# Decode attention with 32 K and V tiles on one core: the output weights' first 16 heads in 20 KB rows, and 0/1 matrices built earlier on GpSimd

## The chip, the core and the metric

One core of a Trainium2 chip runs the whole kernel. The metric is the device time of one execution in microseconds; the figures of a kernel are the median, the lowest and the highest of its runs. Engines: TensorE (PE: matmuls; PEld: its weight loads), VectorE (DVE), ScalarE (ACT), GpSimd (POOL) and SyncE (SP, which here only issues loads). Sixteen DMA engines move the data.

## The reference

One token for each of 8 sequences passes an attention layer with a K and V cache and, beside it, a small MLP. Shapes: D = 640, 32 heads of 128, 4096 keys, F = 1728, all bfloat16.

```python
def _A_ref(x, k_cache, v_cache, wq, wo):
    q = (x @ wq).reshape(B, Sq, Hq, Dh).transpose(0, 2, 1, 3)
    scores = jnp.einsum("bhqd,bhkd->bhqk", q, k_cache) * (Dh ** -0.5)
    p = softmax(scores)
    o = jnp.einsum("bhqk,bhkd->bhqd", p, v_cache)
    return o.transpose(0, 2, 1, 3).reshape(B, Sq, Hq * Dh) @ wo

def _B_ref(x, w1, b1, w2, b2):
    y = _layernorm(x)
    return gelu(y @ w1 + b1) @ w2 + b2

xn = _layernorm(A_x)
return A_x + _A_ref(xn, ...) + _B_ref(xn, ...)
```

The caches hold 8 x 32 x 4096 x 128 values each: 268 MB of K and 268 MB of V. Each is read once.

## The kernel before

**Tiles.** The work is cut into 32 turns (`NQ`). Turn i holds 8 heads (`HS`) of one sequence: i = 8 hq + b, so heads 0 to 7 of all sequences come first and heads 24 to 31 last. A K or V tile of a turn is 128 partitions x 256 keys x 128 values, 8.4 MB, in rows of 64 KB. Partition p holds keys of head p // 16, so eight heads lie side by side in the partitions. There are three slots of this size: KA (K of even turns), KB (K of odd turns) and VS (V of every turn).

**A turn.** K times q is split between two engines. 80 of the 256 keys per partition go over TensorE: `pe_T` transposes them, `act_T` (ScalarE) copies them out of PSUM, `pe_QK` multiplies with q, and `dve_sel` keeps the right head with a mask. The other 176 go over VectorE in three chunks (`dve_chunk`): a product with q in place (`TENSOR_TENSOR`, two operands in SBUF), an add of the two halves (another such), and a reduce over what is left. `dve_max` finds the maxima, `act_exp` makes the exponentials and their sums, `pe_RS` adds the sums over the partitions, `dve_rinv` inverts them, `pe_PV` does 256 matmuls against V, and GpSimd's `o_norm` writes the normalised result of the turn into `oT_sb` (head dimension in the partitions, one column for each head and sequence). The turns overlap: `pe_RS` and `pe_PV` of turn i lie behind the transposes and scores of turn i + 1. In the last turn (31) `o_norm` is done by VectorE.

**Order.** The order of the instructions on each engine is written out by hand. Each step is given a position with `at(pos, fn, ...)`, the steps are sorted by position (turn i begins at 100 i), and each one appends its instructions to the queues of its engines. `o` in the last lines is 3200, behind the last turn. Waits are on semaphores and stand in the queues in the same order, so that an engine that waits holds up all that is behind in its queue.

**GpSimd's queue in a turn.** `qrep` (a copy of q, repeated, 128x128), `o_norm` of the turn before the last, and `k_ready`: a memset of one column that waits for the landing of K and lets TensorE start on it. At its start GpSimd makes constants and iotas (`consts_pool`).

**The output projection.** wo has 4096 rows (32 heads of 128) of 640 values. The contraction runs over the partitions of wo as it is laid out in SBUF. `load_wl(0)` brings heads 0 to 15 as two blocks of 8 heads: in each block partition p holds 8 neighbouring rows of wo, 10 KB in one piece; a block's row p * 8 + s belongs to head p // 16 of the block, at value (p % 16) * 8 + s. `load_wl(1)` brings heads 16 to 23 the same way, and three `load_wn` heads 24 to 31 in three column pieces. They go into the slot KA once K of turn 30 is used up: the waits in `load_wl` are for the last transposes and the last product of K(30) (`tk[("kt", 30)]`, `tk[("km", 30)]`). In SP's queue `load_wl(0)` stands behind V(30) and ahead of the four pieces of V(31); `load_wl(1)` and `load_wn` stand behind those.

Since wo's rows are spread this way, `oT_sb` has to be turned to match: for each s the value (p % 16) * 8 + s of head p // 16 must come to partition p. `sel_pool` (GpSimd) builds 0/1 matrices for this in KA, 8 of 128x128, from the identity. `pe_sel` multiplies them with `oT_sb` of three blocks of heads in four PSUM banks, and `dve_fold` multiplies with a mask (`mask_sb`, one head in 16 partitions) and adds over the heads into `oS_sb`. `pe_sel3` and `dve_fold3` do the same for heads 24 to 31, in two parts: sequences 0 to 6, and, after the last turn, sequence 7. `fin_wl` and `fin_wn` are the projection's matmuls; they add into `ACC_ps`, which already holds x, b2 and the MLP. `fin_store` casts, transposes and stores.

In GpSimd's queue `sel_pool` stands at position 3199, behind the last `o_norm` that GpSimd does (turn 30, position 3175):

Of the kernel before, what the change touches and what calls it, by code (L numbers as in the profile page):

```python
# [14 lines left out]
P = 128  # L15
# [176 lines left out]
def bass_parallel_sum__gqa_block_cached__mixer_channel_mlp__decode_kernel(  # L192
# [17 lines left out]
    HS = 8  # L210
# [13 lines left out]
    KA, KB, VS = 0, 1, 2  # L224
    WL_CUT = (0, 2, 3)
    WN_CUT = (0, 5, 7, HS)
# [21 lines left out]
    with ExitStack() as es:  # L248
# [12 lines left out]
        w1_sb = part(VS, DC * H * DH, DC * F).rearrange("p (c n) -> p c n", c=DC)  # L261
        NL = WL_CUT[-1]
        woL_sb = part(KA, 0, NHQ * HS * D).rearrange("p (g x) -> p g x", g=NHQ)
        sel_sb = part(KA, H * D, HS * P).rearrange("p (c h r) -> p c h r", c=HS, h=HS)
        o_ = [0]
# [16 lines left out]
        iota_h = scratch(2 * HS).bitcast(I32)  # L282
        mtmp = scratch(2 * 2 * HS).bitcast(F32).rearrange("p (w n) -> p w n", w=2)
        ones_sb = scratch(B, 1)
        zeros_sb = scratch(P)
# [8 lines left out]
        oT_sb = sb("oT_sb", [P, H, B], BF)  # L294
        oS_sb = sb("oS_sb", [P, HS, NL, B], BF)
        oS3_sb = sb("oS3_sb", [P, HS, B], BF)
        oU_sb = sb("oU_sb", [P, 2, HS], F32)
        ident_bf = sb("ident_bf", [P, P], BF)
        mask_sb = sb("mask_sb", [P, HS], F32)
        off_sb = sb("off_sb", [P, HS], F32)  # L300
        mx_sb = sb("mx_sb", [P, 32], F32)
# [32 lines left out]
        ld_k0 = _Dma(sem("ld_k0"))  # L334
        ld_wl = [_Dma(sem(f"ld_wl{q}")) for q in range(len(WL_CUT) - 1)]
        ld_wn = [_Dma(sem(f"ld_wn{q}")) for q in range(len(WN_CUT) - 1)]
# [38 lines left out]
        def load_wl(q):  # L375
            sp.wait(tk[("kt", NQ - 2)], tk[("km", NQ - 2)])
            lo, hi = WL_CUT[q], WL_CUT[q + 1]
            n = HS * DH
            tk[("wl", q)] = ld_wl[q].sig(sp.dma_start(
                woL_sb[:, lo:hi, :],  # L380
                A_wo[lo * n:hi * n, :].rearrange("(g p s) n -> p g (s n)", p=P, s=HS)))

        def load_wn(q):
            lo, hi = WN_CUT[q], WN_CUT[q + 1]
            n = HS * DH
            tk[("wn", q)] = ld_wn[q].sig(sp.dma_start(
                woL_sb[:, NL, lo * D:hi * D],
                A_wo[NL * n:(NL + 1) * n, :].rearrange("(p s) n -> p (s n)", p=P)[:, lo * D:hi * D]))

        def consts_pool():  # L390
            pool.iota(iota_h, [[-HP, HS]], base=0, channel_multiplier=1)
            tk["iota"] = pool.sig(pool.iota(iota_i, [[1, P]], base=0, channel_multiplier=-1))
            for d, (ap, v) in zip([None] + ld_vl, (
                    (zeros_sb, 0.0), (ones_sb, 1.0), (mx_sb[:, :], 0.0), (mb_sb[:, :], 0.0))):
                inst = pool.memset(ap, v)
                if d is not None:
                    inst.call[3] = (d.sem, 1)
            tk["consts"] = pool.sig(pool.memset(ones_f[:, :], 1.0))

        def sel_pool():  # L400
            pool.wait(tk["id"], tk[("kt", NQ - 2)], tk[("km", NQ - 2)])
            tk["sel"] = pool.sig(pool.tensor_copy(
                sel_sb[:, :, :, :],
                ident_bf[:, :].rearrange("p (r c) -> p c r", c=HS)[:, :, None, :].to_broadcast([P, HS, HS, HP])))
# [20 lines left out]
        def idents():  # L425
            dve.wait(tk["iota"])
            tk["id"] = dve.sig(dve.tensor_scalar(ident_bf[:, :], iota_i, 0.0, None, ALU.is_equal))
            dve.tensor_scalar(mtmp[:, 0, :], iota_h, 0.0, None, ALU.is_ge)
            t = dve.sig(dve.tensor_scalar(mtmp[:, 1, :], iota_h, float(HP), None, ALU.is_lt))
            dve.wait(t)  # L430
            t = dve.sig(dve.tensor_tensor(mask_sb[:, :], mtmp[:, 0, :], mtmp[:, 1, :], ALU.mult))
            dve.wait(t)
            tk["mask"] = dve.sig(dve.tensor_scalar(off_sb[:, :], mask_sb[:, :], 1.0, 1e30, ALU.subtract, ALU.mult))

        def pe_xT(w):
# [237 lines left out]

        def pe_sel(n):
            ap, bank = sel_bank(n)
            pe.wait(tk["sel"], *[tk[("on", i)] for i in range(NL * B)])
            bank.use(pe)
            w = HS * B
            for x in range(2 * NL):
                c, g = divmod(x, NL)  # L680
                last = pe.matmul(ap[:, x * w:(x + 1) * w],
                                 sel_sb[:, 2 * n + c, :, :].rearrange("p h r -> p (h r)"),
                                 oT_sb[:, g * HS:(g + 1) * HS, :].rearrange("p h b -> p (h b)"),
                                 start=True, stop=True)
            bank.used(pe, pe.sig(last))

        def dve_fold(n):
            ap, bank = sel_bank(n)
            bank.use(dve)
            view = ap[:, 0:2 * NL * HS * B].rearrange("p (x h b) -> p x h b", h=HS, b=B)  # L690
            t = dve.sig(dve.tensor_tensor(
                view, view, mask_sb[:, None, :, None].to_broadcast([P, 2 * NL, HS, B]), ALU.mult))
            dve.wait(t)
            tk[("oS", n)] = bank.used(dve, dve.sig(dve.tensor_reduce(
                oS_sb[:, 2 * n:2 * n + 2, :, :].rearrange("p s g b -> p (s g) b"),
                view.rearrange("p x h b -> p x b h"), AX.X, ALU.add)))

        def sel3_b(n):
            return (0, B - 1, QB_ps[:, :], QBB) if n == 0 else (B - 1, B, S_ps[:, 0, :], SBK[0])

        def pe_sel3(n):
            lo, hi, ap, bank = sel3_b(n)
            pe.wait(tk["sel"], *[tk[("on", NL * B + b)] for b in range(lo, hi)])
            bank.use(pe)
            view = ap[:, 0:HS * HS * (hi - lo)].rearrange("p (h s b) -> p h s b", h=HS, s=HS)
            for c in range(HS):
                last = pe.matmul(view[:, :, c, :], sel_sb[:, c, :, :].rearrange("p h r -> p (h r)"),
                                 oT_sb[:, NL * HS:H, lo:hi], start=True, stop=True)
            bank.used(pe, pe.sig(last))

        def dve_fold3(n):
            lo, hi, ap, bank = sel3_b(n)
            w = HS * (hi - lo)
            bank.use(dve)
            view = ap[:, 0:HS * w].rearrange("p (h x) -> p h x", h=HS)
            t = dve.sig(dve.tensor_tensor(
                view, view, mask_sb[:, :, None].to_broadcast([P, HS, w]), ALU.mult))
            dve.wait(t)
            tk[("oS3", n)] = bank.used(dve, dve.sig(dve.tensor_reduce(
                oS3_sb[:, :, lo:hi], view.rearrange("p h (s b) -> p s b h", s=HS), AX.X, ALU.add)))  # L720

        def fin_wl(q):
            lo, hi = WL_CUT[q], WL_CUT[q + 1]
            pe.wait(tk[("wl", q)], *[tk[("oS", n)] for n in range(HS // 2)])
            for g in range(lo, hi):
                for r in range(HS):
                    for c in range(DC):
                        pe.matmul(ACC_ps[:, c * B:(c + 1) * B], woL_sb[:, g, r * D + c * P:r * D + (c + 1) * P],
                                  oS_sb[:, r, g, :], start=False, stop=False, skip_group_check=True)

        def fin_wn(q):
            lo, hi = WN_CUT[q], WN_CUT[q + 1]
            pe.wait(tk[("wn", q)], tk[("oS3", 0)], tk[("oS3", 1)])
            for r in range(lo, hi):
                for c in range(DC):
                    last = pe.matmul(ACC_ps[:, c * B:(c + 1) * B],
                                     woL_sb[:, NL, r * D + c * P:r * D + (c + 1) * P], oS3_sb[:, r, :],
                                     start=False, stop=(r == HS - 1), skip_group_check=True)
# [27 lines left out]
        at(-795, idents)  # L766
        at(NQ * Q - 1, sel_pool)
        at(-790, norm, 0)
        at(-780, pe_xT, 0)
        at(-775, cp_xT, 0)  # L770
        at(-774, norm, 1)
# [40 lines left out]
        o = NQ * Q  # L812
        for q in range(len(WL_CUT) - 1):
            at(o - 55 if q == 0 else o + 50 + 0.1 * q, load_wl, q)
            at(o + 79.1 + 0.2 * q, fin_wl, q)
        for q in range(len(WN_CUT) - 1):
            at(o + 51 + q, load_wn, q)
            at(o + 80 + q, fin_wn, q)
        for n in range(HS // 2):
            at(o + n, pe_sel, n)  # L820
            at(o + 0.5 + n, dve_fold, n)
        for n in range(2):
            at(o + 5 if n == 0 else o + 79.2, pe_sel3, n)
            at(o + 5.5 if n == 0 else o + 79.5, dve_fold3, n)
        at(o + 90, fin_store)
# [72 lines left out]
```

## Time and profile before

| | |
|---|---|
| median of 3 runs | 1283.74 us (1283.46 to 1283.85) |
| profiled execution: time | 1283.28 us |
| profiled execution: span | 1281.7 us |
| TensorE's granted clock, mean | 0.588 |
| read from HBM | 551.80 MB, 431 GB/s over the span |
| busy share: DMA engines, nearly every slice | 0.9 or more |
| busy: VectorE | 1094.9 us (85%) |
| busy: TensorE matmuls | 669.8 us (52%) |
| busy: ScalarE | 475.5 us (37%) |
| busy: GpSimd | 92.1 us (7%) |
| K(31) lands, VectorE starts on it | 1227.32 us |
| last wo piece that the chain of waits names lands | 1277.36 us |

The span goes from the first to the last instruction of the program on the core; the time of an execution holds some more around it (1.6 us here). Times below with two decimals are microseconds from the span's start. In a line of the timeline stand: start, duration, engine, line, operation, output <- inputs, shapes, number of instructions, and in brackets the idle time of the engine just before, with what ended it. All of the work has line 111, that of a helper which records every operation, so operations are told apart by their tiles. `S_sb` is the memory of the three slots, so K, V and all that is put into them for a time (the weights, the 0/1 matrices) bear that name.

### The profile page before, as it was taken

How to read it: one execution, taken by the hardware profiler on the slowest of the kernel's cores; microseconds unless marked ns; L12 is line 12 of the kernel's file. 1: busy time of each engine (PE TensorE's matmuls, PEld its weight loads, DVE VectorE, ACT ScalarE, POOL GpSimd, SP SyncE). 2: the span in 40 equal slices, each digit the busy share in tenths (PEclk: the TensorE clock that was granted, in tenths of full speed). 3: DMA queues.
4: the chain of work that ended last, by engine and by line, in shares of the span. 5: the costliest groups of instructions: out<-in, count | busy, mean ns of one | idle time of the engine just before them, and what ended most of it. 6: DMA issues, size and time to landing. Idle time of an engine off the chain costs nothing.

```text
span 1281.7 us, 34444 instructions
## 1 busy us (share of the span) xinstructions
PE 669.8 (52%) x13944; PEld 572.4 (45%) x13944; DVE 1094.9 (85%) x675; ACT 475.5 (37%) x904; POOL 92.1 (7%) x108
## 2 busy tenths in 40 slices
PE   4365554564544564544664644654544654545655
PEld 4354443453443453433553533543434544434545
DVE  1799988988888988888988888988889988889885
ACT  1344432344432344423344423344423344323441
POOL 0001100000000000000000000000000000000001
PEclk9956555566555656556666556656556566555655
DMA  9999999999999999999999999999999999999998
GB/s 401 443 427 426 442 432 432 430 442 430 434 430 442 430 434 430 442 427 436 427 444 427 436 427 444 427 434 430 442 428 434 432 442 427 432 434 440 430 418 368
DMA packets 11235, 551.99 MB, mean 431 GB/s; under 512 B 1292, under 2 KB 1493, under 8 KB 1878
## 3 DMA queue, kind: packets, MB, share of 16 engines
q1 hardware_dynamic: 11072, 551.70, 99.6%
q8 instruction: 9, 0.15, 0.0%
q10 hardware_dynamic: 150, 0.11, 0.0%
q14 instruction: 4, 0.03, 0.0%
HBM read 551.80 MB, written 0.01 MB: 431 GB/s over the span
## 4 chain that ended last, share of the span: by engine, by line
DMA 80%; PE 19%; issue 1%; ACT 0%; SPq 0%; another core or an unknown queue 0%; DVE 0%; POOL 0%; ACTq 0%
DMA S_sb<-in_A_v_cache_dram 74%; PE PV_ps L111 17%; DMA S_sb<-in_A_k_cache_dram 3%; DMA S_sb<-in_A_wo_dram 2%; DMA S_sb<-in_B_w_dram 2%; PE TR_ps L111 1%; PE CH_ps L111 1%; ACT P_sb L111 0%; PE ACC_ps L111 0%; PE S_ps L111 0%; SPq L111 0%; ACT KT_sb L111 0%; PE QB_ps L111 0%; ACT S_sb L111 0%
## 5 line engine op out<-in xcount | busy, mean ns | idle before, releaser
L111 PE MATMUL TR_ps<-ident_bf,S_sb 128*128 128x128 bf16 (+1 forms) x2570 | 340.9, 271 | 376.2 <-POOL kr_sb L111 368.6
L111 DVE TENSOR_TENSOR S_sb<-S_sb,qbc_sb 128x7552 bf16<-128x7552 bf16 (+1 forms) x96 | 388.7, 4049 | 135.8 <-DMA S_sb<-in_A_k_cache_dram 135.8
L111 PEld LDWEIGHTS TR_ps<-ident_bf,S_sb 128*128 (+2 forms) x2570 | 244.4, 103 | 435.4 <-issue 359.8
L111 DVE TENSOR_REDUCE Sd_sb<-S_sb 128x59 f32<-128x3776 bf16 (+1 forms) x96 | 390.2, 4065 | 6.0
L111 ACT ACTIVATE KT_sb<-TR_ps 128x1024 bf16<-128x1024 bf16 x320 | 327.2, 1024 | 123.8 <-PE TR_ps L111 111.3
L111 PE MATMUL PV_ps<-P_sb,S_sb 128*128 128x8 bf16 x8192 | 224.0, 175 | 151.4 <-DMA S_sb<-in_A_v_cache_dram 147.9
L111 PEld LDWEIGHTS PV_ps<-P_sb,S_sb 128*128 128x128 bf16 x8192 | 221.2, 103 | 154.3 <-DMA S_sb<-in_A_v_cache_dram 150.7
L111 ACT ACTIVATE P_sb<-Sd_sb,NB_sb 128x256 bf16<-128x256 f32 x256 | 126.2, 494 | 219.2 <-DVE NB_sb L111 219.2
L111 DVE TENSOR_TENSOR S_sb<-S_sb 128x3776 bf16<-128x3776 bf16 (+1 forms) x96 | 202.9, 2114 | 3.3
L111 ACT ACTIVATE oU_sb<-PV_ps 128x8 f32<-128x8 f32 x31 | 5.5, 178 | 393.3 <-PE PV_ps L111 393.3
L111 PE MATMUL S_ps<-qrep_sb,KT_sb 128*128 128x8 bf16 x2560 | 122.0, 178 | 35.5 <-ACT KT_sb L111 32.2
L111 PEld LDWEIGHTS S_ps<-qrep_sb,KT_sb 128*128 128x128 bf16 x2560 | 91.1, 102 | 66.4 <-ACT KT_sb L111 37.6
L111 POOL TENSOR_TENSOR oT_sb<-oU_sb,ri_sb 128x8 bf16<-128x8 f32 x31 | 68.8, 2220 | 387.0 <-DVE S_sb L111 363.9
L111 POOL COPY qrep_sb<-qT_sb 128x128 bf16<-128x128 bf16 x32 | 17.2, 536 | 456.3 <-PE S_ps L111 436.1
L111 ACT ACTIVATION_READ_ACCUMULATOR P_sb<-Sd_sb,NB_sb 128x1 f32 x256 | 47.8, 187 | 0.0
L111 DVE TENSOR_TENSOR S_ps<-S_ps,mask_sb 128x320 f32<-128x320 f32 (+2 forms) x67 | 32.7, 487 | 4.7 <-PE S_ps L111 4.7
L111 DVE TENSOR_REDUCE Sd_sb<-S_ps 128x40 f32<-128x320 f32 x64 | 31.4, 491 | 2.2
L111 POOL MEMSET kr_sb<- 128x1 f32 x32 | 3.2, 99 | 322.0 <-DMA S_sb<-in_A_k_cache_dram 322.0
L111 PE MATMUL QB_ps<-ident_bf,qrep_sb 128*128 128x128 bf16 x32 | 9.1, 284 | 22.5 <-DVE S_sb L111 21.4
L111 PE MATMUL CH_ps<-rs_sb,ones_f 128*128 128x8 f32 x64 | 15.4, 314 | 9.9 <-DVE oS_sb L111 6.2
L111 ACT ACTIVATE qbc_sb<-QB_ps 128x128 bf16<-128x128 f32 x32 | 8.9, 277 | 27.6 <-PE QB_ps L111 27.6
L111 PEld LDWEIGHTS CH_ps<-rs_sb,ones_f 128*128 128x128 f32 x64 | 13.2, 258 | 10.1 <-DVE TR_ps L111 6.3
(57 smaller groups left out, 119.2 us busy)
## 6 DMA issues: line engine op xcount, KB each, us to landing
S_sb<-in_A_wq_dram SPq DMA_DIRECT2D x1, 5120.0 KB, 16.0
S_sb<-in_A_k_cache_dram SPq DMA_DIRECT2D x1, 4448.0 KB, 43.7
S_sb<-in_A_v_cache_dram SPq DMA_DIRECT2D x2, 2048.0 KB, 13.3
S_sb<-in_A_k_cache_dram SPq DMA_DIRECT2D x1, 3744.0 KB, 34.0
S_sb<-in_A_v_cache_dram SPq DMA_DIRECT2D x1, 3584.0 KB, 14.6
S_sb<-in_A_wo_dram SPq DMA_DIRECT2D x1, 2560.0 KB, 31.2
S_sb<-in_B_w_dram SPq DMA_DIRECT2D x1, 2160.0 KB, 20.7
S_sb<-in_B_w_dram SPq DMA_DIRECT2D x1, 2080.0 KB, 25.5
```

The source lines that it names most:

```text
L111: inst = getattr(e, name)(*a, **k)
```

## The change

wo's heads 0 to 15 are loaded as one block of 16 heads: partition p holds 16 neighbouring rows, 20 KB in one piece, and belongs to head p // 8. The turning of these heads is done by 16 matrices of 128x128 (`selW_sb`), a mask with one head in 8 partitions (`maskw_sb`) and an output `oW_sb`: `pe_selw` and `dve_foldw`, 4 matrices in each of four banks. Heads 16 to 23 are turned by the old matrices and the old fold, in one part, in the bank `QB_ps` (`pe_sel(2, 0)`); heads 24 to 31 as before, in the same bank behind it. VectorE folds heads 16 to 23 first, then the four banks of the 16 heads. GpSimd builds both sets of matrices at position 3140 instead of one at 3199: behind `k_ready` of turn 31 (3098) and ahead of `o_norm` of turn 30 (3175). The iota and the mask for 16 heads are made at the start, by GpSimd and VectorE. The loads keep their places in SP's queue.

```diff
-    WL_CUT = (0, 2, 3)
+    HW = 16
+    RW = P // HW
+    NL = 3
...
-        NL = WL_CUT[-1]
-        woL_sb = part(KA, 0, NHQ * HS * D).rearrange("p (g x) -> p g x", g=NHQ)
-        sel_sb = part(KA, H * D, HS * P).rearrange("p (c h r) -> p c h r", c=HS, h=HS)
+        woW_sb = part(KA, 0, HW * D)
+        woL_sb = part(KA, HW * D, 2 * HS * D).rearrange("p (g x) -> p g x", g=2)
+        selW_sb = part(KA, H * D, HW * P).rearrange("p (c h r) -> p c h r", c=HW, h=HW)
+        sel_sb = part(KA, H * D + HW * P, HS * P).rearrange("p (c h r) -> p c h r", c=HS, h=HS)
...
+        iota_w = scratch(2 * HW).bitcast(I32)
+        mtmpw = scratch(2 * 2 * HW).bitcast(F32).rearrange("p (w n) -> p w n", w=2)
...
+        oW_sb = sb("oW_sb", [P, HW, B], BF)
+        oS_sb = sb("oS_sb", [P, HS, B], BF)
...
+        maskw_sb = sb("maskw_sb", [P, HW], F32)
...
         def load_wl(q):
             sp.wait(tk[("kt", NQ - 2)], tk[("km", NQ - 2)])
-            lo, hi = WL_CUT[q], WL_CUT[q + 1]
-            n = HS * DH
+            lo, hi = (0, HW) if q == 0 else (HW, HW + HS)
             tk[("wl", q)] = ld_wl[q].sig(sp.dma_start(
-                woL_sb[:, lo:hi, :],
-                A_wo[lo * n:hi * n, :].rearrange("(g p s) n -> p g (s n)", p=P, s=HS)))
+                woW_sb if q == 0 else woL_sb[:, 0, :],
+                A_wo[lo * DH:hi * DH, :].rearrange("(p s) n -> p (s n)", p=P)))
 
         def load_wn(q):
             lo, hi = WN_CUT[q], WN_CUT[q + 1]
             n = HS * DH
             tk[("wn", q)] = ld_wn[q].sig(sp.dma_start(
-                woL_sb[:, NL, lo * D:hi * D],
+                woL_sb[:, 1, lo * D:hi * D],
                 A_wo[NL * n:(NL + 1) * n, :].rearrange("(p s) n -> p (s n)", p=P)[:, lo * D:hi * D]))
 
         def consts_pool():
             pool.iota(iota_h, [[-HP, HS]], base=0, channel_multiplier=1)
+            pool.iota(iota_w, [[-RW, HW]], base=0, channel_multiplier=1)
             tk["iota"] = pool.sig(pool.iota(iota_i, [[1, P]], base=0, channel_multiplier=-1))
             for d, (ap, v) in zip([None] + ld_vl, (
                     (zeros_sb, 0.0), (ones_sb, 1.0), (mx_sb[:, :], 0.0), (mb_sb[:, :], 0.0))):
@@ -399,6 +406,9 @@
 
         def sel_pool():
             pool.wait(tk["id"], tk[("kt", NQ - 2)], tk[("km", NQ - 2)])
+            tk["selw"] = pool.sig(pool.tensor_copy(
+                selW_sb[:, :, :, :],
+                ident_bf[:, :].rearrange("p (r c) -> p c r", c=HW)[:, :, None, :].to_broadcast([P, HW, HW, RW])))
             tk["sel"] = pool.sig(pool.tensor_copy(
                 sel_sb[:, :, :, :],
                 ident_bf[:, :].rearrange("p (r c) -> p c r", c=HS)[:, :, None, :].to_broadcast([P, HS, HS, HP])))
@@ -431,6 +441,12 @@
             t = dve.sig(dve.tensor_tensor(mask_sb[:, :], mtmp[:, 0, :], mtmp[:, 1, :], ALU.mult))
             dve.wait(t)
             tk["mask"] = dve.sig(dve.tensor_scalar(off_sb[:, :], mask_sb[:, :], 1.0, 1e30, ALU.subtract, ALU.mult))
+
+        def maskw():
+            dve.tensor_scalar(mtmpw[:, 0, :], iota_w, 0.0, None, ALU.is_ge)
+            t = dve.sig(dve.tensor_scalar(mtmpw[:, 1, :], iota_w, float(RW), None, ALU.is_lt))
+            dve.wait(t)
+            dve.tensor_tensor(maskw_sb[:, :], mtmpw[:, 0, :], mtmpw[:, 1, :], ALU.mult)
 
         def pe_xT(w):
             src = xn_sb if w == 0 else y_sb
@@ -671,70 +687,69 @@
         def sel_bank(n):
             return (S_ps[:, n, :], SBK[n]) if n < 2 else (TR_ps[:, n - 2, :].bitcast(F32), TRB[n - 2])
 
-        def pe_sel(n):
+        def pe_selw(n):
             ap, bank = sel_bank(n)
-            pe.wait(tk["sel"], *[tk[("on", i)] for i in range(NL * B)])
+            pe.wait(tk["selw"], *[tk[("on", i)] for i in range(2 * B)])
             bank.use(pe)
-            w = HS * B
-            for x in range(2 * NL):
-                c, g = divmod(x, NL)
+            w = HW * B
+            for x in range(4):
                 last = pe.matmul(ap[:, x * w:(x + 1) * w],
-                                 sel_sb[:, 2 * n + c, :, :].rearrange("p h r -> p (h r)"),
-                                 oT_sb[:, g * HS:(g + 1) * HS, :].rearrange("p h b -> p (h b)"),
-                                 start=True, stop=True)
+                                 selW_sb[:, 4 * n + x, :, :].rearrange("p h r -> p (h r)"),
+                                 oT_sb[:, 0:HW, :].rearrange("p h b -> p (h b)"), start=True, stop=True)
             bank.used(pe, pe.sig(last))
 
-        def dve_fold(n):
+        def dve_foldw(n):
             ap, bank = sel_bank(n)
             bank.use(dve)
-            view = ap[:, 0:2 * NL * HS * B].rearrange("p (x h b) -> p x h b", h=HS, b=B)
+            view = ap.rearrange("p (x h b) -> p x h b", h=HW, b=B)
             t = dve.sig(dve.tensor_tensor(
-                view, view, mask_sb[:, None, :, None].to_broadcast([P, 2 * NL, HS, B]), ALU.mult))
-            dve.wait(t)
-            tk[("oS", n)] = bank.used(dve, dve.sig(dve.tensor_reduce(
-                oS_sb[:, 2 * n:2 * n + 2, :, :].rearrange("p s g b -> p (s g) b"),
-                view.rearrange("p x h b -> p x b h"), AX.X, ALU.add)))
-
-        def sel3_b(n):
+                view, view, maskw_sb[:, None, :, None].to_broadcast([P, 4, HW, B]), ALU.mult))
+            dve.wait(t)
+            tk[("oW", n)] = bank.used(dve, dve.sig(dve.tensor_reduce(
+                oW_sb[:, 4 * n:4 * n + 4, :], view.rearrange("p x h b -> p x b h"), AX.X, ALU.add)))
+
+        def sel_b(g, n):
+            if g == 2:
+                return (0, B, QB_ps[:, :], QBB)
             return (0, B - 1, QB_ps[:, :], QBB) if n == 0 else (B - 1, B, S_ps[:, 0, :], SBK[0])
 
-        def pe_sel3(n):
-            lo, hi, ap, bank = sel3_b(n)
-            pe.wait(tk["sel"], *[tk[("on", NL * B + b)] for b in range(lo, hi)])
+        def pe_sel(g, n):
+            lo, hi, ap, bank = sel_b(g, n)
+            pe.wait(tk["sel"], *[tk[("on", g * B + b)] for b in range(lo, hi)])
             bank.use(pe)
             view = ap[:, 0:HS * HS * (hi - lo)].rearrange("p (h s b) -> p h s b", h=HS, s=HS)
             for c in range(HS):
                 last = pe.matmul(view[:, :, c, :], sel_sb[:, c, :, :].rearrange("p h r -> p (h r)"),
-                                 oT_sb[:, NL * HS:H, lo:hi], start=True, stop=True)
+                                 oT_sb[:, g * HS:(g + 1) * HS, lo:hi], start=True, stop=True)
             bank.used(pe, pe.sig(last))
 
-        def dve_fold3(n):
-            lo, hi, ap, bank = sel3_b(n)
+        def dve_fold(g, n):
+            lo, hi, ap, bank = sel_b(g, n)
             w = HS * (hi - lo)
             bank.use(dve)
             view = ap[:, 0:HS * w].rearrange("p (h x) -> p h x", h=HS)
             t = dve.sig(dve.tensor_tensor(
                 view, view, mask_sb[:, :, None].to_broadcast([P, HS, w]), ALU.mult))
             dve.wait(t)
-            tk[("oS3", n)] = bank.used(dve, dve.sig(dve.tensor_reduce(
-                oS3_sb[:, :, lo:hi], view.rearrange("p h (s b) -> p s b h", s=HS), AX.X, ALU.add)))
+            tk[("oS", g, n)] = bank.used(dve, dve.sig(dve.tensor_reduce(
+                (oS_sb if g == 2 else oS3_sb)[:, :, lo:hi], view.rearrange("p h (s b) -> p s b h", s=HS),
+                AX.X, ALU.add)))
 
         def fin_wl(q):
-            lo, hi = WL_CUT[q], WL_CUT[q + 1]
-            pe.wait(tk[("wl", q)], *[tk[("oS", n)] for n in range(HS // 2)])
-            for g in range(lo, hi):
-                for r in range(HS):
-                    for c in range(DC):
-                        pe.matmul(ACC_ps[:, c * B:(c + 1) * B], woL_sb[:, g, r * D + c * P:r * D + (c + 1) * P],
-                                  oS_sb[:, r, g, :], start=False, stop=False, skip_group_check=True)
+            pe.wait(tk[("wl", q)], *([tk[("oW", n)] for n in range(4)] if q == 0 else [tk[("oS", 2, 0)]]))
+            w, o, rows = (woW_sb, oW_sb, HW) if q == 0 else (woL_sb[:, 0, :], oS_sb, HS)
+            for r in range(rows):
+                for c in range(DC):
+                    pe.matmul(ACC_ps[:, c * B:(c + 1) * B], w[:, r * D + c * P:r * D + (c + 1) * P],
+                              o[:, r, :], start=False, stop=False, skip_group_check=True)
 
         def fin_wn(q):
             lo, hi = WN_CUT[q], WN_CUT[q + 1]
-            pe.wait(tk[("wn", q)], tk[("oS3", 0)], tk[("oS3", 1)])
+            pe.wait(tk[("wn", q)], tk[("oS", 3, 0)], tk[("oS", 3, 1)])
...
@@ -764,9 +779,10 @@
         at(-870, load_k, 0)
         at(-800, consts_pool)
         at(-795, idents)
-        at(NQ * Q - 1, sel_pool)
+        at(NQ * Q - 60, sel_pool)
         at(-790, norm, 0)
         at(-780, pe_xT, 0)
+        at(-776, maskw)
         at(-775, cp_xT, 0)
         at(-774, norm, 1)
         at(-773, pe_xT, 1)
@@ -810,18 +826,21 @@
         at(71, act_O, -1)
         at(75, o_norm, -1)
         o = NQ * Q
-        for q in range(len(WL_CUT) - 1):
+        for q in range(2):
             at(o - 55 if q == 0 else o + 50 + 0.1 * q, load_wl, q)
             at(o + 79.1 + 0.2 * q, fin_wl, q)
         for q in range(len(WN_CUT) - 1):
             at(o + 51 + q, load_wn, q)
             at(o + 80 + q, fin_wn, q)
-        for n in range(HS // 2):
-            at(o + n, pe_sel, n)
-            at(o + 0.5 + n, dve_fold, n)
-        for n in range(2):
-            at(o + 5 if n == 0 else o + 79.2, pe_sel3, n)
-            at(o + 5.5 if n == 0 else o + 79.5, dve_fold3, n)
+        at(o + 4.5, pe_sel, 2, 0)
+        at(o + 5.05, dve_fold, 2, 0)
+        for n in range(4):
+            at(o + 0.1 * n, pe_selw, n)
+            at(o + 5.1 + 0.1 * n, dve_foldw, n)
+        at(o + 5.2, pe_sel, 3, 0)
+        at(o + 5.7, dve_fold, 3, 0)
+        at(o + 79.2, pe_sel, 3, 1)
+        at(o + 79.5, dve_fold, 3, 1)
         at(o + 90, fin_store)
         engs = {"dve": dve, "act": act}
         marks = {n: [] for n in engs}
```

More of the change, by code (lines that the diff above doesn't have):

```diff
@@ L294, in bass_parallel_sum__gqa_block_cached__mixer_channel_mlp__decode_kernel @@
         oT_sb = sb("oT_sb", [P, H, B], BF)
-        oS_sb = sb("oS_sb", [P, HS, NL, B], BF)
+        oW_sb = sb("oW_sb", [P, HW, B], BF)
+        oS_sb = sb("oS_sb", [P, HS, B], BF)
         oS3_sb = sb("oS3_sb", [P, HS, B], BF)
@@ L334, in bass_parallel_sum__gqa_block_cached__mixer_channel_mlp__decode_kernel @@
         ld_k0 = _Dma(sem("ld_k0"))
-        ld_wl = [_Dma(sem(f"ld_wl{q}")) for q in range(len(WL_CUT) - 1)]
+        ld_wl = [_Dma(sem(f"ld_wl{q}")) for q in range(2)]
         ld_wn = [_Dma(sem(f"ld_wn{q}")) for q in range(len(WN_CUT) - 1)]
@@ L736, in fin_wn @@
                     last = pe.matmul(ACC_ps[:, c * B:(c + 1) * B],
-                                     woL_sb[:, NL, r * D + c * P:r * D + (c + 1) * P], oS3_sb[:, r, :],
+                                     woL_sb[:, 1, r * D + c * P:r * D + (c + 1) * P], oS3_sb[:, r, :],
                                      start=False, stop=(r == HS - 1), skip_group_check=True)
```

## The prediction

> **What bounds the kernel now.** I read the page's chain of work first, then the chain of waits over the last 40 us, and then the engines' timelines there, because the change works only at the start and in the last 60 us. The page's summary of the chain:
>
> ```profile
> DMA 80%; PE 19%; issue 1%; ACT 0%; SPq 0%; another core or an unknown queue 0%; DVE 0%; POOL 0%; ACTq 0%
> ...
> HBM read 551.80 MB, written 0.01 MB: 431 GB/s over the span
> ```
>
> The kernel is a stream of loads. Its end, in the chain of waits from 1240 us (start, duration, what):
>
> ```profile
> 1254.95 22.41 DMA S_sb<-in_A_wo_dram
> 1277.36 0.04 issue
> 1277.40 1.50 PE ACC_ps L111 x40
> ```
>
> The last wo pieces (`load_wn`) land at 1277.36; 40 matmuls of `fin_wn` and the store follow. Beside that runs a second path, which ends almost as late. TensorE's timeline at the end:
>
> ```profile
> 1266.07 0.56 PE L111 MATMUL CH_ps<-rs_sb,ones_f 128*128 128x8 f32 x2 [6.16 <-DVE oS_sb L111]
> 1266.49 6.97 PE L111 MATMUL PV_ps<-P_sb,S_sb 128*128 128x8 bf16 x256
> 1273.46 2.28 PE L111 MATMUL ACC_ps<-oS_sb,S_sb 128*128 128x8 bf16 x80
> 1275.59 0.36 PE L111 MATMUL S_ps<-oT_sb,S_sb 128*128 128x8 bf16 x8
> 1275.81 1.21 PE L111 MATMUL ACC_ps<-oS_sb,S_sb 128*128 128x8 bf16 x40
> 1277.40 1.49 PE L111 MATMUL ACC_ps<-oS_sb,S_sb 128*128 128x8 bf16 x40 [0.39 <-DMA S_sb<-in_A_wo_dram]
> ```
>
> TensorE stands idle for 0.39 us before the last group, and that group is itself stretched by two more landings: 40 matmuls at PV's pace (7.0 us / 256 = 27 ns) are 1.09 us. Without waits it would end at 1277.02 + 1.09 = 1278.11 instead of 1278.90. So the compute path has a slack of 0.8 us, no more. What sets the compute path is VectorE, busy without a hole from the landing of the last K on; lines of its timeline:
>
> ```profile
> 1227.32 4.03 DVE L111 TENSOR_TENSOR S_sb<-S_sb,qbc_sb 128x7424 bf16<-128x7424 bf16 x1 [4.25 <-DMA S_sb<-in_A_k_cache_dram]
> 1231.38 2.09 DVE L111 TENSOR_TENSOR S_sb<-S_sb 128x3712 bf16<-128x3712 bf16 x1
> 1233.59 4.02 DVE L111 TENSOR_REDUCE Sd_sb<-S_sb 128x58 f32<-128x3712 bf16 x1
> 1237.53 4.08 DVE L111 TENSOR_TENSOR S_sb<-S_sb,qbc_sb 128x7552 bf16<-128x7552 bf16 x1
> ...
> 1261.52 0.23 DVE L111 TENSOR_SCALAR NB_sb<-off_sb,mbT_sb 128x8 f32<-128x8 f32 x1
> 1261.70 0.57 DVE L111 TENSOR_TENSOR S_ps<-S_ps,mask_sb 128x384 f32<-128x384 f32 x1
> ```
>
> The chain is: K(31) lands 1227.3, three chunks and the maxima to 1261.75, eight exps to 1265.8, PV(31) 1266.49 to 1273.46, projection. Whatever VectorE loses between 1227 and 1261 moves PV(31) by as much, and all beyond 0.8 us the end.
>
> **What GpSimd does there now.** Its timeline (end of the run, and two rows of the turn before):
>
> ```profile
> 1202.49 0.58 POOL L111 COPY qrep_sb<-qT_sb 128x128 bf16<-128x128 bf16 x1 [13.84 <-PE S_ps L111]
> 1215.19 2.19 POOL L111 TENSOR_TENSOR oT_sb<-oU_sb,ri_sb 128x8 bf16<-128x8 f32 x1 [12.12 <-DVE S_sb L111]
> 1227.26 0.10 POOL L111 MEMSET kr_sb<- 128x1 f32 x1 [9.87 <-DMA S_sb<-in_A_k_cache_dram]
> 1253.90 2.17 POOL L111 TENSOR_TENSOR oT_sb<-oU_sb,ri_sb 128x8 bf16<-128x8 f32 x1 [26.54 <-DVE S_sb L111]
> 1255.99 1.98 POOL L111 COPY S_sb<-ident_bf 128x1024 bf16<-128x1024 bf16 x1
> ```
>
> Eight elements take 2.19 us at 1215.19: VectorE's add of two SBUF operands ran from 1215.17 to 1217.29, and GpSimd finished at 1217.38, 0.09 us behind it. The `qrep` copy asked at 1202.49, inside VectorE's product (1198.84 to 1202.92), and ended at 1203.07, 0.15 us behind that product, although the next add began at 1202.96. So GpSimd gets nothing while a VectorE instruction with two SBUF inputs runs, and slips in between two of them. The old 0/1 copy lies beside a reduce (one SBUF input): neither is slowed.
>
> **The change, part by part.**
>
> *The load.* wo's heads 0 to 15 come as 128 rows of 20,480 bytes instead of 256 of 10,240. The trace's packets give 389 ns for 10,240 bytes and 2421 for 65,536, a line with 12.7 ns fixed per packet. Each of 16 engines has 8 packets fewer: 8 x 12.7 = 0.10 us off the stream. That is all this part can give; it is issued at the same place in SP's queue (behind V(30), 1221.49).
>
> *Start.* One more iota (GpSimd, 0.14 us by the 128x8 row) and three small VectorE operations (about 0.17 each, 0.5 in all) before the copy of x's transpose, which ends at 8.38. The first projection waits for wq until 16.81: hidden, 8.4 us of cover; without it, 0.6.
>
> *Turning.* TensorE: 16 matmuls of 128 columns, 8 of 64 and 8 of 56 in place of 24 of 64 and 8 of 56, all after PV(30) at 1253.6, where it now waits 4.42 us for GpSimd and afterwards idles until 1266. No cost: some 2 us in 12 us of idleness. New: the turn of heads 24 to 31 waits for the fold of heads 16 to 23 (same bank), and is ahead of the row sums and PV(31) in TensorE's queue. That fold is VectorE's first after the maxima (done 1.3 us after 1261.75), the exps take 4.1: cover 2.1 us after the 0.6 of the eight matmuls.
>
> *Folds.* Rows: 384 columns cost 0.57 + 0.56, spaced 1.07 a pair; 448 cost 1.20 a pair; hence 512 cost 1.33. Five pairs of 512 and one of 448 are 7.85 us against 5.47: +2.4, ending at 1269.6 instead of 1267.2. The next use is PV(31)'s end at 1273.46: hidden by PV, 3.9 us to spare.
>
> *Projection.* 80 + 40 + 40 matmuls as before: 0.
>
> *GpSimd's queue.* The builds are moved ahead of the last but one `o_norm`: behind the memset that waits for K(31) (1227.26), ahead of 1253.9. They are a 128x2048 copy (`selW_sb`) and the known 128x1024 one. Their own wait (K(30) used up, 1221.5) is past. Behind them stands only that `o_norm`, which needs PV(30) at 1253.6; both copies end before 1240: no cost there. But now they start together with VectorE's product of K(31) at 1227.32, not beside a reduce. Length: 128 elements unhindered take 0.29 us (the first `qrep`), 1024 take 1.98, so 1.89 ns an element and 3.92 for 2048. By the `qrep` row the copy gets in when the product ends at 1231.35, 0.15 us completes its first 128 elements and 1920 x 1.89 = 3.63 us the others: it ends at 1235.13. VectorE's add, due at 1231.38, is then running against it.
>
> What the add loses is not in the trace: no row shows VectorE behind a long GpSimd copy (the 0.15 us copies cost the adds nothing, 2.12 with and without). Bounds: 0, if VectorE has precedence or both take turns, and the whole rest, 3.75 us, if the port is held for an instruction, as GpSimd's 2.19 us for eight elements look from the other side. I take 3.75. A gain is excluded: nothing is taken off VectorE there.
> The Trainium skill, "SBUF — State Buffer", section "Who interferes with whom", states that rule: a VectorE instruction with two SBUF inputs and a GpSimd instruction that reads SBUF exclude each other for the whole instruction, the first to start blocking the other. The trace agrees for GpSimd (2.19 us); for VectorE no row of before shows it. By that rule the sum is the one below, without it that of the first rival.
>
> **The sum.** Delay 3.75, less 0.8 slack: +2.95. Against the profiled execution (span 1281.7, time 1283.28, so 1.6 outside the span): span 1284.6, time 1286.2. The median of the runs is 1283.74, 0.46 above the profiled one: 1286.7. The copy's length may be 3.6 to 4.0 (from a larger fixed part to twice 1.98): 1286.3 to 1286.8 and, with the slack uncertain by 0.3, 1286.0 to 1287.1 as its own range.
> The Trainium skill, "GPSIMD Engine Reference", section "Performance pitfalls for Q7 kernels", gives about 2.9 instead of 1.9 cycles an element where the step read exceeds 8 bytes, as both copies' does; an estimate from it, at its 1.2 GHz, is 2.4 ns and 1287.7. The row's 1.89 ns, at a step of 16 bytes, does not show that.
>
> **Rivals.**
> 1. No block (the other side): VectorE is not held by a running copy. For: the 2.12 us adds after `qrep`. Against: those copies end before the add needs the port. Then the load stream sets the end, 0.1 us sooner: 1283.6. It decides if the add at 1231.38 takes under 2.9 us.
> 2. Both copies pass before the add: the second copy has no wait and, as at 1255.99, starts 0.08 before the one ahead of it ends. 1.93 more, delay 5.7, less 0.8: 1288.6. Against: VectorE has been asking for 3.7 us by then.
> 3. The copy goes by rows, not elements: 64 rows of 16 become 256 of 8. (1.98 - 0.29) / 56 = 30 ns a row, 7.8 us in all, delay 7.6: 1290.5.
> 4. GpSimd misses the 0.03 us gap and copies beside the reduce: 1233.5 to 1237.25; then the second copy stands before the product due at 1237.53 until 1239.2: delay 1.7, +0.9: 1284.6. Against: all `qrep` rows use the gap.
> 5. Faster: the load saves 0.1, and the compute path, unshortened, allows 0.8 at most.
>
> **Chances.** Forecast 0.42; no block 0.20; both copies 0.24; rows 0.07; reduce 0.06; faster by over 0.2% 0.01. A measurement of this kernel tells some 0.2% (2.6 us) from no change. The forecast's +2.95 is near that bound: seven in ten of it lie beyond. Slower: 0.29 + 0.24 + 0.07 = 0.60; faster 0.02; same 0.38. The range, 1283.4 to 1289.3, holds all but the rows case and the tails.
>
> **What would show it.** Right: the add after the first product of K(31) takes some 5.8 us instead of 2.09, and a 128x2048 copy of 3.9 us of its own (about 7.8 with its wait) ends where the add gets going; PV(31) starts near 1270.2; the last 40 matmuls wait for no DMA; the chain of waits runs through VectorE back to K(31). Wrong: that add unchanged at 2.09, or the copies beside reduces alone; a second VectorE stall of 2 us (rival 2). A PV(31) that starts at 1266.5 with an end at 1281.6 means that nothing but the load mattered.

## The result, and the profile after

The changed kernel takes 1288.04 us (median of 7 runs, 1287.96 to 1288.59) against 1283.61 (7 runs, 1283.39 to 1283.85): +4.4 us, ratio 1.0035 (95% interval 1.0024 to 1.0047), so it is slower. The prediction said 1286.7, in a range of 1283.4 to 1289.3, and slower with a chance of 0.60. Its profiled execution took 1287.96 us, with a span of 1286.3.

VectorE's timeline of the changed kernel around the last K (start, duration, engine, line, operation), then GpSimd's in the same stretch:

```profile
1227.38 7.74 DVE L111 TENSOR_TENSOR S_sb<-S_sb,qbc_sb 128x7424 bf16<-128x7424 bf16 x1 [4.25 <-DMA S_sb<-in_A_k_cache_dram]
1235.15 3.80 DVE L111 TENSOR_TENSOR S_sb<-S_sb 128x3712 bf16<-128x3712 bf16 x1
1239.08 4.02 DVE L111 TENSOR_REDUCE Sd_sb<-S_sb 128x58 f32<-128x3712 bf16 x1
1243.01 4.08 DVE L111 TENSOR_TENSOR S_sb<-S_sb,qbc_sb 128x7552 bf16<-128x7552 bf16 x1
```

```profile
1227.32 0.10 POOL L111 MEMSET kr_sb<- 128x1 f32 x1 [9.87 <-DMA S_sb<-in_A_k_cache_dram]
1227.36 3.88 POOL L111 COPY S_sb<-ident_bf 128x2048 bf16<-128x2048 bf16 x1
...
1231.17 5.83 POOL L111 COPY S_sb<-ident_bf 128x1024 bf16<-128x1024 bf16 x1
```

The product of K(31) takes 7.74 us instead of 4.03, the add 3.80 instead of 2.09. The larger build starts at 1227.36, 0.02 us ahead of the product, and ends at 1231.24; the product ends 3.88 us later, nearly its own length of 4.03: it did next to nothing while the copy ran. The second build asks at 1231.17 and gets nothing until the product is done at 1235.12; then it goes for 1.88 us, and the add starts behind it. The reduce (4.02) and all that VectorE does behind it, up to the maxima, have their old durations. The loss is 3.71 + 1.71 = 5.42 us. With the slack of 0.8 us at the end taken off, that is 4.6: the spans of the two profiled executions differ by 4.6 us, the medians by 4.4.

TensorE's timeline of the changed kernel at the end:

```profile
1268.76 0.59 PE L111 MATMUL QB_ps<-oT_sb,S_sb 128*128 128x56 bf16 x8 [11.57 <-DVE oS_sb L111]
1271.57 0.57 PE L111 MATMUL CH_ps<-rs_sb,ones_f 128*128 128x8 f32 x2 [2.22 <-ACT P_sb L111]
1271.99 6.98 PE L111 MATMUL PV_ps<-P_sb,S_sb 128*128 128x8 bf16 x256
1278.96 2.28 PE L111 MATMUL ACC_ps<-oW_sb,S_sb 128*128 128x8 bf16 x80
1281.10 0.36 PE L111 MATMUL S_ps<-oT_sb,S_sb 128*128 128x8 bf16 x8
1281.31 2.27 PE L111 MATMUL ACC_ps<-oS_sb,S_sb 128*128 128x8 bf16 x80
```

PV(31) starts 5.5 us later than before. The last 80 matmuls run as one piece, with no wait for a load: all of wo has long landed. In the chain of waits the end no longer hangs on wo but, through the exps and VectorE, on K(31):

```profile
1182.84 44.43 DMA S_sb<-in_A_k_cache_dram
...
1227.38 7.75 DVE S_sb L111
1235.15 3.81 DVE S_sb L111
...
1267.28 4.04 ACT P_sb L111 x16
```

The load did what was reckoned. The packet count on the page of the profile fell by 128, from 11235:

```profile
DMA packets 11107, 551.99 MB, mean 429 GB/s; under 512 B 1292, under 2 KB 1493, under 8 KB 1878
```

A packet of 20,480 bytes took 765 ns (two of 10,240: 778), so 8 x 13 = 0.10 us for each engine.

### The profile page after: what moved, and what is told of

The parts are those of the page before. It is cut to its first block, busy times and chain, and to the rows that moved or that the text cites. A ratio compares the mean times of both kernels' runs of the same rounds, so it can differ in the third digit from the quotient of the medians.

```text
span 1286.3 us, 34450 instructions
## 1 busy us (share of the span) xinstructions
PE 671.1 (52%) x13944; PEld 574.8 (45%) x13944; DVE 1103.2 (86%) x680; ACT 475.5 (37%) x904; POOL 97.3 (8%) x110
## 4 chain that ended last, share of the span: by engine, by line
DMA 55%; DVE 32%; issue 10%; PE 1%; ACT 1%; DVEq 0%; SPq 0%; POOL 0%; ACTq 0%
DMA S_sb<-in_A_k_cache_dram 55%; DVE S_sb L111 24%; DVE Sd_sb L111 6%; DVE S_ps L111 1%; ACT KT_sb L111 1%; PE PV_ps L111 1%; PE ACC_ps L111 0%; ACT P_sb L111 0%; DVE ri_sb L111 0%; DVEq L109 0%; PE TR_ps L111 0%; SPq L111 0%; PE S_ps L111 0%; DVE mx_sb L111 0%; PE CH_ps L111 0%
## 5 line engine op out<-in xcount | busy, mean ns | idle before, releaser
L111 POOL COPY qrep_sb<-qT_sb 128x128 bf16<-128x128 bf16 x32 | 14.0, 436 | 455.5 <-PE S_ps L111 435.7
L111 DVE TENSOR_TENSOR S_ps<-S_ps,mask_sb 128x320 f32<-128x320 f32 (+1 forms) x65 | 31.6, 486 | 3.9 <-PE S_ps L111 3.9
```

The source lines that it names most:

```text
L111: inst = getattr(e, name)(*a, **k)
```

## The experiments

In all of them the kernel before, run beside them, had a median of 1283.53 to 1283.61.

**Builds back at their old place.**

```diff
-        at(NQ * Q - 60, sel_pool)
+        at(NQ * Q - 1, sel_pool)
```

> The changed kernel with both builds back behind GpSimd's last o_norm (position 3199), all else as changed. Theory (the builds hold the port that VectorE's product and add of K(31) need): product 4.03 us and add 2.09 us again, the builds from 1256.0 to 1261.8 beside a reduce, TensorE's turning from 1260 instead of 1254.5, folds done by 1271, before PV(31)'s end at 1273.5; time 1283.5, up to 1284.5 if the small operations on the maxima are held by the second build. Rival (the larger folds, the bank shared by two turnings, the start or the load cost the time): stays near 1288.

Measured: 1283.43 us (1283.25 to 1283.75), ratio 0.9998 (0.9989 to 1.0007). VectorE's timeline in this run:

```profile
1227.88 4.02 DVE L111 TENSOR_TENSOR S_sb<-S_sb,qbc_sb 128x7424 bf16<-128x7424 bf16 x1 [4.26 <-DMA S_sb<-in_A_k_cache_dram]
1231.94 2.09 DVE L111 TENSOR_TENSOR S_sb<-S_sb 128x3712 bf16<-128x3712 bf16 x1
...
1261.62 0.77 DVE L111 TENSOR_SCALAR mb_sb<-mq_sb 128x32 f32<-128x32 f32 x1
```

Product and add have their old lengths, and with them the whole loss is gone: folds, masks, banks and load cost nothing that can be measured. The builds ran from 1256.55 to 1262.35 here, beside a reduce and the maxima; one operation on the maxima was held, 0.77 us instead of 0.18, inside the slack. The late place is not free either: here, and in the memset run below, which builds at the same place, the chain of waits runs through the builds, and PV(31) starts 39.77 us behind the product of K(31) instead of 39.17 (1267.65 against 1227.88). That is 0.6 us of the 0.8 us of slack.

**The move alone, in the kernel before** (one build of 128x1024, the old load and folds).

```diff
-        at(NQ * Q - 1, sel_pool)
+        at(NQ * Q - 60, sel_pool)
```

> The kernel before with one edit: its one build of 128x1024 moved from position 3199 to 3140. Theory: it starts 0.02 us ahead of the product of K(31) and holds it for its 1.98 us less 0.16 (the loss of the product in the changed kernel was 3.72 for a copy of 3.88): product 5.85 us, add 2.09; delay 1.8 less 0.8 us of slack, +1.0: 1284.6. Rival (copies of this length cost VectorE nothing): 1283.6. Rival (no slack at the end): 1285.4.

Measured: 1284.57 us (1284.41 to 1284.84), ratio 1.0007 (0.9998 to 1.0017): +1.04 by the medians. VectorE's timeline, and GpSimd's copy:

```profile
1227.60 5.84 DVE L111 TENSOR_TENSOR S_sb<-S_sb,qbc_sb 128x7424 bf16<-128x7424 bf16 x1 [4.25 <-DMA S_sb<-in_A_k_cache_dram]
1233.48 2.09 DVE L111 TENSOR_TENSOR S_sb<-S_sb 128x3712 bf16<-128x3712 bf16 x1
```

```profile
1227.58 1.98 POOL L111 COPY S_sb<-ident_bf 128x1024 bf16<-128x1024 bf16 x1
```

The copy again begins 0.02 us ahead of the product, which then takes 1.81 us more. 1.81 - 1.04 leaves 0.8 us of slack at the end, as reckoned from the trace of before. The interval of this experiment alone reaches below 1; the product's duration is what shows the hold.

**Builds ahead of K(31), while VectorE waits for it** (their own semaphore, since TensorE's loop counts the other one in equal steps).

```diff
-        at(NQ * Q - 60, sel_pool)
+        at(NQ * Q - 103, sel_pool)
-            tk["selw"] = pool.sig(pool.tensor_copy(
+            tk["selw"] = pool2.sig(pool.tensor_copy(
-            tk["sel"] = pool.sig(pool.tensor_copy(
+            tk["sel"] = pool2.sig(pool.tensor_copy(
```

> The changed kernel with both builds ahead of the memset that waits for K(31) (position 3097, on a semaphore of their own): they lie in the 4.25 us in which VectorE waits for K(31). Theory: copies from 1221.5 to 1227.3, product 4.03 to 4.15 us, add 2.09; the load stream sets the end again: 1283.5. Rival (the other parts of the change cost the time): near 1288. Rival (the builds hold back the small operations on the maxima of turn 30 and so PV(30) and the load of V(31)): above 1284.5, with PV(30) starting after 1246.7.

Measured: 1283.45 us (1283.27 to 1283.76), ratio 1.0 (0.999 to 1.0009); product 4.02, add 2.09. VectorE's timeline just ahead of K(31):

```profile
1222.14 0.21 DVE L111 STREAM_TRANSPOSE mxT_sb<-mx_sb 128x32 f32<-128x32 f32 x1
1222.38 0.19 DVE L111 TENSOR_REDUCE mq_sb<-mxT_sb 128x2 f32<-128x32 f32 x1
1222.60 3.00 DVE L111 TENSOR_SCALAR mb_sb<-mq_sb 128x32 f32<-128x32 f32 x1
1225.64 0.21 DVE L111 STREAM_TRANSPOSE mbT_sb<-mb_sb 128x32 f32<-128x32 f32 x1
1225.88 1.62 DVE L111 TENSOR_SCALAR NB_sb<-off_sb,mbT_sb 128x8 f32<-128x8 f32 x1
1227.54 4.02 DVE L111 TENSOR_TENSOR S_sb<-S_sb,qbc_sb 128x7424 bf16<-128x7424 bf16 x1
```

The copies ran from 1221.71 to 1227.48. They held two operations on the maxima of turn 30 (3.00 for 0.18, 1.62 for 0.23) but not the reduces and transposes beside them, and all of that fell into the 4.25 us in which VectorE would have waited for K(31), with nothing to spare: the second held operation ended at 1227.50, 0.04 us ahead of the product. The first of the two reads a single tile, so two inputs in SBUF are not the only case in which VectorE is held.

**The builds asking 0.5 us later**, behind a memset, so that the product is first.

```diff
             pool.wait(tk["id"], tk[("kt", NQ - 2)], tk[("km", NQ - 2)])
+            pool.memset(part(KA, H * D + HW * P + HS * P, 512), 0.0)
```

> The changed kernel with a memset of 128x512 in unused memory ahead of the two builds, so that they ask for the port some 0.3 us later, after VectorE's product has begun. Theory (who asks first has the port for one instruction, then the one that waits gets it): product 4.03 us, add 2.09 + 3.7 = 5.8 us, the second build beside the reduce; delay 3.75 less 0.8, 1286.4. Rival (GpSimd keeps the port from one copy to the next): add 7.7 us, 1288.2. Rival (whoever starts first does not matter, only the length of the copies): 1288.0.

Measured: 1286.31 us (1286.08 to 1286.58), ratio 1.0021 (1.0012 to 1.003). VectorE's timeline, then GpSimd's:

```profile
1227.58 4.03 DVE L111 TENSOR_TENSOR S_sb<-S_sb,qbc_sb 128x7424 bf16<-128x7424 bf16 x1 [4.25 <-DMA S_sb<-in_A_k_cache_dram]
1231.64 5.68 DVE L111 TENSOR_TENSOR S_sb<-S_sb 128x3712 bf16<-128x3712 bf16 x1
```

```profile
1228.02 7.35 POOL L111 COPY S_sb<-ident_bf 128x2048 bf16<-128x2048 bf16 x1
...
1235.31 3.90 POOL L111 COPY S_sb<-ident_bf 128x1024 bf16<-128x1024 bf16 x1
```

This is the course of events that the prediction described: product untouched, copy in the gap behind it, add held by 3.59 us, VectorE served ahead of the second copy, which then runs beside the reduce. Half a microsecond more of GpSimd's time, spent ahead of the copies, made the kernel 1.7 us faster than the changed one.

**GpSimd busy there, but only writing:** the builds late, two memsets of 128x4608 at their early place.

```diff
+        def mem_pool():
+            pool.wait(tk["id"], tk[("kt", NQ - 2)], tk[("km", NQ - 2)])
+            for n in range(2):
+                pool.memset(part(KA, H * D + HW * P + HS * P + n * 4608, 4608), 0.0)
...
-        at(NQ * Q - 60, sel_pool)
+        at(NQ * Q - 60, mem_pool)
+        at(NQ * Q - 1, sel_pool)
```

> As the kernel with both builds back at 3199, but with two memsets of 128x4608 in unused memory at position 3140, where the changed kernel builds: GpSimd is busy there about as long (0.82 ns an element by a 128x512 memset of 0.52 us, so 3.9 us each), and writes SBUF without reading it. Theory A (the product and the add hold against GpSimd's reads alone): product 4.03 us, add 2.09, time 1283.5. Theory B (any GpSimd instruction holds them): product 7.7, add 3.8 to 5.8, time 1288 or more.

Measured: 1283.47 us (1283.31 to 1283.8), ratio 1.0 (0.999 to 1.0009). GpSimd's first memset, and VectorE's product and add:

```profile
1227.53 3.94 POOL L111 MEMSET S_sb<- 128x4608 bf16 x1
```

```profile
1227.56 4.03 DVE L111 TENSOR_TENSOR S_sb<-S_sb,qbc_sb 128x7424 bf16<-128x7424 bf16 x1 [4.25 <-DMA S_sb<-in_A_k_cache_dram]
1231.62 2.09 DVE L111 TENSOR_TENSOR S_sb<-S_sb 128x3712 bf16<-128x3712 bf16 x1
```

The memset is ahead of the product by 0.03 us and as long as the copy, and the product keeps its length. So theory A holds: it is GpSimd's reading of SBUF that holds the product, not its being busy.

**Beside the reduces.** Each build waits for an add of K(31).

```diff
-            pool.wait(tk["id"], tk[("kt", NQ - 2)], tk[("km", NQ - 2)])
+            pool.wait(tk["id"], tk[("kt", NQ - 2)], tk[("ya", NQ - 1, 0)])
             tk["selw"] = pool.sig(pool.tensor_copy(
...
+            pool.wait(tk[("ya", NQ - 1, 1)])
             tk["sel"] = pool.sig(pool.tensor_copy(
```

> The changed kernel with the builds at the same place in GpSimd's queue, but each waiting for an add of K(31): the build for 16 heads for that of the first chunk, the other for that of the second. They run beside the reduces, which read one operand from SBUF. Theory: reduces 4.02 and 4.09 us as ever, product of the second chunk late by 0.1 at most (the copy of 3.88 ends 0.1 us ahead of it), time 1283.5. Rival (the larger copy reaches into the next product and holds it): up to +0.5 on that product, still inside the slack: 1283.6. Rival (a copy slows a reduce as well): a reduce of 6 us or more, 1285.5.

Measured: 1283.55 us (1283.26 to 1283.69), ratio 1.0 (0.999 to 1.0009). The copies took 3.91 and 1.98 us, the reduces beside them 4.02 and 4.09, products and adds were untouched.

**In 24 pieces of 128x128**, at the changed kernel's place.

```diff
+            for c in range(HW):
+                tk["selw"] = pool.sig(pool.tensor_copy(
+                    selW_sb[:, c, :, :],
+                    ident_bf[:, :].rearrange("p (r c) -> p c r", c=HW)[:, c, None, :].to_broadcast([P, HW, RW])))
...
```

> The changed kernel with the builds at the same place, cut into 24 copies of 128x128 (16 and 8 matrices). Theory (the port is held for one instruction and then goes to the one that waits): the first copy holds the product by 0.1 to 0.3 us, one copy slips in behind it and holds the add by as much, the others run beside the reduce, some 0.25 to 0.3 us each; delay 0.6 at most, inside the slack: 1283.5. Rival (what counts is the sum of the copying): product and add as in the changed kernel, 1288. Rival (a row of copies without waits keeps the port): product above 6 us, 1286 or more.

Measured: 1286.45 us (1286.23 to 1286.82), ratio 1.0022 (1.0013 to 1.0032): the theory failed, if not at the start; the time is that of the second rival (a row of copies without waits keeps the port, as these texts call what the two engines contend for), by another product than it named. VectorE's timeline:

```profile
1227.31 4.27 DVE L111 TENSOR_TENSOR S_sb<-S_sb,qbc_sb 128x7424 bf16<-128x7424 bf16 x1 [4.25 <-DMA S_sb<-in_A_k_cache_dram]
1231.61 2.19 DVE L111 TENSOR_TENSOR S_sb<-S_sb 128x3712 bf16<-128x3712 bf16 x1
1233.92 4.02 DVE L111 TENSOR_REDUCE Sd_sb<-S_sb 128x58 f32<-128x3712 bf16 x1
1237.85 7.56 DVE L111 TENSOR_TENSOR S_sb<-S_sb,qbc_sb 128x7552 bf16<-128x7552 bf16 x1
```

The first product and add lose 0.24 and 0.10, a piece each, as expected, although the next piece was queued without a wait. Then the pieces run in a row beside the reduce, 0.41 us each, one every 0.35, and the next product, which asks at 1237.85 in the middle of the row, is held to the end of it at 1241.47.

**A row of longer copies, and the pieces apart.** Two runs ask what kept VectorE out. The first puts ten copies of 128x512 in a row behind the first add of K(31) (four of them into unused memory), the second lets each piece of 128x128 wait for the one ahead.

```diff
+            for n in range(4):
+                tk["selw"] = pool.sig(pool.tensor_copy(
+                    selW_sb[:, 4 * n:4 * n + 4, :, :],
+                    idw[:, 4 * n:4 * n + 4, None, :].to_broadcast([P, 4, HW, RW])))
...
```

> The builds beside the first reduce of K(31), cut into copies of 128x512 (4 and 2), with four more such copies into unused memory behind them, none waiting for the one ahead: a row of ten copies of some 1.0 us from 1233.6 to 1243.5. The product of the second chunk asks at 1237.7, in the middle of the row. Theory A (VectorE gets the port at the end of any copy): the product loses 1.0 us at most, one copy slips in before the add and costs it as much, the others run beside the reduce: delay 2.0 less 0.8, at most 1284.8. Theory B (a row of copies that is already under way keeps the port, as the ten pieces did): the product is held to the end of the row, loss about 5.8, 1288.5. If A holds, it was the shortness of the pieces of 128 that kept VectorE out.

```diff
             for c in range(HW):
+                pool.wait(tk.get("selw"))
...
             for c in range(HS):
+                pool.wait(tk.get("sel", tk["selw"]))
...
```

> The 24 pieces of 128x128 at the changed kernel's place, each waiting for the semaphore of the one ahead, so that GpSimd lets the port go between them. Theory B (what keeps the port is that the next copy begins before the last one ends): product 4.3 us, add 2.2, some nine pieces beside the reduce, the second product held 0.4 us at most, its add 0.1: delay 0.9, 1283.7. Rival (VectorE misses the gaps between short pieces all the same): second product 7 us or more, 1286.4 or more.

Measured: the row of longer copies 1283.66 us (ratio 1.0, 0.9989 to 1.001), the pieces apart 1283.54 (1.0, 0.999 to 1.0009). VectorE's timeline with the longer copies, and with the pieces apart:

```profile
1237.81 4.22 DVE L111 TENSOR_TENSOR S_sb<-S_sb,qbc_sb 128x7552 bf16<-128x7552 bf16 x1
1242.07 2.89 DVE L111 TENSOR_TENSOR S_sb<-S_sb 128x3776 bf16<-128x3776 bf16 x1
```

```profile
1238.13 4.08 DVE L111 TENSOR_TENSOR S_sb<-S_sb,qbc_sb 128x7552 bf16<-128x7552 bf16 x1
1242.25 2.21 DVE L111 TENSOR_TENSOR S_sb<-S_sb 128x3776 bf16<-128x3776 bf16 x1
```

In the row of longer copies VectorE is served at the end of the copy that is running (0.14 lost, then 0.77 for the one copy that slips in ahead of the add). Apart, the short pieces cost 0.24, 0.10 and 0.09. So a row as such does not keep the port, nor do short pieces as such. Short pieces in a row without waits did, once the row had been running beside the reduce for some 4 us; VectorE had got in after the first and the second piece of that same row. Why is open.

## Why the prediction was right, and where it was not

- **The number.** The direction and what causes it were right. The forecast's own range, 1286.0 to 1287.1, was missed by 0.9 us; that 1288.04 lies in the wide range is owed to the room left there for rival 2, not to the course of events that the forecast described. Of its signs of being right, the last 40 matmuls without a wait and the chain through VectorE to K(31) came; an add of 5.8 us and PV(31) at 1270.2 did not (3.80 us and 1271.99), and a second stall of nearly 2 us, named as a sign against it, did.
- **What bounds the kernel.** Right. The load stream sets the end in the kernel before, and four kernels that leave product and add of the first chunk alone (late, ahead, memset, beside the reduces) come out between 1283.43 and 1283.55. In two of them, ahead and beside the reduces, the chain of waits ends on wo again; in the other two it runs through the late builds, inside the slack. The compute path's slack of 0.8 us is what the move alone showed (1.81 lost, 1.04 paid).
- **The load.** 0.10 us predicted and in the packets. In the time it can't be told: 0.10 and 0.08 less than before with the builds late and ahead, with intervals from 0.9989 to 1.0009.
- **Start, turning, folds, projection.** Hidden, as said. The five pairs of 512 columns and one of 448 took 7.98 us (1267.19 to 1275.17; predicted 7.85), PV(31) covered them; the turning that waits for the first fold was done at 1269.35, 2.2 us ahead of the row sums (the predicted cover was 2.1).
- **The copies' length.** 3.92 us predicted for 2048 elements, 3.88 measured; the price by rows of the third rival is out. The estimate from the Trainium skill's "GPSIMD Engine Reference", "Performance pitfalls for Q7 kernels", was too dear: the copy's step of 32 bytes costs the same 1.9 ns an element as that of 16.
- **That VectorE is held.** Right, and it was the term for which the trace of before had no row. Undoing it in three ways (late, ahead, beside the reduces) takes the whole loss away, and memsets at the changed kernel's place bring none of it back. The rule in the Trainium skill, "SBUF — State Buffer", "Who interferes with whom", stands: two SBUF inputs of VectorE against a GpSimd instruction that reads, and not against one that only writes; the memset run shows the second half. Two things seen here go beyond these two cases: an operation with a single input tile was held as well (3.00 us for 0.18), and a row of short copies kept VectorE out to its end, for which no run gives the reason.
- **Which instruction is held: the step that failed.** "By the `qrep` row the copy gets in when the product ends at 1231.35." `qrep` asks in the middle of a product; the build follows a memset that is released by the same landing of K(31) as the product, and was 0.02 us ahead of it, here and in the run with the move alone. So the first copy cost the product 3.71 us, and the second, which was to lie beside the reduce, found the gap between product and add and cost 1.71. The delay was 5.42, not 3.75. With the product first, the kernel takes 1286.31, and the predicted 1286.7 is that case. The delay of 3.75 was thus right in kind and reckoned for one copy, where two held VectorE.
- **Rival 2** (both copies, 1288.6) had nearly the right time, and both copies did run before the add got going, but by another way: the second copy did not keep the port, VectorE got it in between. What spoke against it, that VectorE has been asking all along, was right.

## What to carry to other kernels

An engine with 7% of busy time can still cost the end, through what it shares: before a long GpSimd copy is moved, look which VectorE instructions lie beside it at the new place, and put it beside reduces or into VectorE's waits for a load. A short delay that lets VectorE begin only lessened the loss here, from 4.4 to 2.8 us. Work that is released by the same event as the critical instruction races with it, and 0.02 us decided over 1.7. And if a load stream sets the end, price larger rows by the packets that they save: here 0.1 us, too little to be seen in the time.

## What the runs showed of the hardware that was not expected

- A product or add with two SBUF operands waits for a GpSimd copy from start to end (7.74 us behind a copy of 3.88), and the port then goes to the side that waits: with copies of 1.0 us and more VectorE was served at the end of the one running, although the next copy is recorded as starting some 0.06 us before that end.
- The last ten of a row of copies of 0.41 us without waits held one product by 3.48 us (7.56 for 4.08); with a semaphore wait between the copies VectorE lost 0.24 at most. What makes the difference was not found.
- Float32 operations with a scalar on 32 and 8 columns were held like the large products (3.00 us for 0.18, 1.62 for 0.23), while reduces and 32x32 transposes next to them were not.
